# Top-k attention's mask and exponential as two ScalarE passes, the scaling on GpSimd, silu's product on VectorE

## The chip, the cores and the metric

The kernel runs on one core of a Trainium2 chip. Its time is the device time of one execution in microseconds (us). The engines are named as the profile names them: PE (TensorE matmul; PEld is its weight load), DVE (VectorE), ACT (ScalarE), POOL (GpSimd) and SP (SyncE, which issues the DMAs). Each engine works through its own queue in order; semaphores make one wait for another.

## The reference, cut to what matters

Three parts follow each other. The first is attention of 16 heads over 576 positions, in which each row of scores keeps its 32 largest:

```python
scores = scale * q @ k.T
kth = 32nd largest of each row
scores = where(scores >= kth, scores, -1e9) - rowmax
attn = exp(scores); attn /= attn.sum(-1) + 1e-9
x = attn @ v                             # 1152 tokens x 512
h = x @ w_in                             # 512 -> 2048, the "m" part
x = (h * sigmoid(h)) @ w_out             # silu, 2048 -> 512
P = sinkhorn(exp(x @ w_gate))            # 1152 tokens x 8 experts
out = sum_e P[:, e] * (relu(x @ w1[e]) @ w2[e])
```

## The kernel before

The 1152 tokens are cut into nine tiles of 128, and these into five groups: group 0 has tile 0, groups 1 to 4 have two tiles each. For each group the attention runs over four pairs of heads, and then the m part of the group (m0 to m4: 16 blocks of the 2048 hidden columns each). From 620 us on eight experts follow, on PE alone at its pace.

**One score tile** (`score_tile`, L314) is 128 rows by 576 scores. There are 8 in group 0 and 64 in groups 1 to 4; of these eight (names ending in h) serve the odd half tiles of group 2. PE forms the scores (L320, `ps`), ACT copies them to `s` (L323), then DVE finds the 32 largest in four rounds: MAX8 (L332, `m8`) finds eight, MATCH_REPLACE8 (L339) strikes them out in `w`. Beside that ACT computes `e = exp(scale*s - scale*max)` (L337), as soon as the first round has given the row's maximum and `tiny` (POOL from group 1 on) has scaled it (L335, `sm`). After the fourth round DVE multiplies `e` with `s >= kth` into `s` and sums it (L342), `tiny` adds 1e-9 (L344), DVE takes the reciprocal (L345), ACT scales `s` (L347). PE transposes the result in five pieces (L350, L352, `pt`), ACT copies them to `aT` (L363, L364), and PE multiplies by v (L360, `pav`).

**silu** in `step` (L447 to L454): with t = tanh(h/2), silu(h) = (t+1)*h/2. ACT computes t (L447); for m1 and m4 DVE forms (t+1)*h in one instruction from PSUM (L449); for m2 and m3 ACT copies h (L451) and adds 1 to t (L452), and POOL multiplies (L453). `split` (L135) then parts a float32 array in a high and a low half: ACT writes the high one (L137), POOL or DVE the difference (L138).

**What sets the order.** The code gives each instruction a priority; a scheduler (Tile's, with a timeline of its own) lays them out on the five queues ahead of time. The work of groups has priority; `FILL` hands out low-priority filler for PE that needs no attention result of a later group: experts 0 to 7 for tile 0 (`row_ffn`: L598, L609, L614, L617, with four splits of 128x512 each by ACT and POOL for one block), and expert 0 for tiles 1 to 4. The m part of group g runs while DVE is in group g+1. The first m part that runs in blocks, m1, splits its weights on the way (two splits of 128x512 per block); m2 to m4 load what it kept.

`tc.issue_after(behind.ins)` keeps the instructions in its scope behind `opened`, the evacuation of the first token tile after m0, for the four tiles of group 1's first pair. Five buffers hold `s` (SB).

The lines that the change touches are these, with what calls them.

Of the kernel before, what the change touches and what calls it, by code (L numbers as in the profile page):

```python
# [8 lines left out]
F32 = mybir.dt.float32  # L9
# [3 lines left out]
AF = mybir.ActivationFunctionType  # L13
ALU = mybir.AluOpType
# [3 lines left out]
P = 128  # L18
TOPK = 32
# [53 lines left out]
def topk_attention_moe_sinkhorn_kernel(  # L73
# [12 lines left out]
    nc = tc.nc  # L86
    B, H, S, D = q.shape
# [6 lines left out]
    NTT = NT // P  # L94
    SH = S // 2
    SCALE = 1.0 / D ** 0.5
    MASKED = -1e9 / SCALE
    W = DM
    assert NDC * P == W

# [7 lines left out]
    const = ctx.enter_context(tc.tile_pool(name="const", bufs=1))  # L108
# [1 line left out]
    make_identity(nc, ident)  # L110
    ones = const.tile([P, P], F32, name="ones")
    nc.gpsimd.memset(ones, 1.0)
    neg = const.tile([P, 1], F32, name="neg")
    nc.gpsimd.memset(neg, MASKED)
    wg_raw = const.tile([P, NDC, NE], F32, name="wg_raw")
    wgH = const.tile([P, NDC, NE], F32R, name="wgH")
    wgL = const.tile([P, NDC, NE], F32R, name="wgL")
# [78 lines left out]
    sp = att.enter_context(tc.tile_pool(name="sp", bufs=SW))  # L196
# [116 lines left out]
    def score_tile(nm, qq, qL, kk, js, cols, soon, behind=None, late=False):  # L313

        ps = ps_s.tile([P, 2, 512], F32, name=f"ps_{nm}", tag="s")

        for j in js:
            for part, a in enumerate((qq, qL)):
                for hh in range(2):
                    nc.tensor.matmul(ps[:, hh, 0:SH], a[:, j, cols], kk[:, j, hh * SH : (hh + 1) * SH],  # L320
                                     start=j == js[0] and part == 0, stop=j == js[-1] and part == 1)
        s = sp.tile([P, S], F32, name=f"s_{nm}", tag="s", bufs=SB)
        copied.append(nc.scalar.activation(s.rearrange("p (a c) -> p a c", a=2), ps[:, :, 0:SH], AF.Copy))  # L323
        w = sp.tile([P, S], F32, name=f"w_{nm}", tag="w")
        m8 = small.tile([P, TOPK], F32, name=f"m8_{nm}", tag="m8")
        sm = small.tile([P, 4], F32, name=f"sm_{nm}", tag="sm")
        e = sp.tile([P, S], F32, name=f"e_{nm}", tag="e")
        src = s
        tiny = nc.vector if soon else nc.gpsimd
        for r in range(TOPK // 8):  # L330
            mr = m8[:, 8 * r : 8 * r + 8]
            nc.vector.max(mr, src)  # L332
            if r == 0:

                tiny.tensor_scalar(sm[:, 0:1], m8[:, 0:1], -SCALE, None, op0=ALU.mult)  # L335
                with tc.issue_after(behind.ins) if behind and late else nullcontext():
                    nc.scalar.activation(e, s, AF.Exp, scale=SCALE, bias=sm[:, 0:1])  # L337
            if r < TOPK // 8 - 1:
                nc.vector.match_replace(out=w, in_to_replace=mr, in_values=src, imm_value=-3e38)  # L339
                src = w  # L340

        nc.vector.scalar_tensor_tensor(s, s, m8[:, TOPK - 1 : TOPK], e, op0=ALU.is_ge, op1=ALU.mult,  # L342
                                       accum_out=sm[:, 1:2])
        tiny.tensor_scalar(sm[:, 2:3], sm[:, 1:2], 1e-9, None, op0=ALU.add)  # L344
        normal.append(nc.vector.reciprocal(sm[:, 3:4], sm[:, 2:3]))  # L345
        with tc.issue_after(behind.ins) if behind else nullcontext():
            nc.scalar.activation(s, s, AF.Copy, scale=sm[:, 3:4])  # L347
        pt = ps_t.tile([P, 4, P], F32, name=f"pt_{nm}", tag="tr")
# [73 lines left out]
    def step(pend, nm, xs, ys, wa, wb, first, last, silu, ph, pool, late=False, depth=2, done=None, half=False):  # L422
# [3 lines left out]
        ph = ph[:, :N]  # L426
# [16 lines left out]
        if silu:  # L443

            g = hp.tile([P, W], F32, name=f"g_{nm}", tag="g")[:, :N]
            t = hp.tile([P, W], F32, name=f"t_{nm}", tag="t")[:, :N]
            nc.scalar.activation(t, ph, AF.Tanh, scale=0.5)  # L447
            if late or nm.startswith("m1"):
                nc.vector.scalar_tensor_tensor(g, t, 1.0, ph, op0=ALU.add, op1=ALU.mult)  # L449
            else:  # L450
                nc.scalar.activation(g, ph, AF.Copy)  # L451
                nc.scalar.activation(t, t, AF.Copy, bias=1.0)  # L452
                nc.gpsimd.tensor_mul(g, t, g)  # L453
            split(gH, gL, g, nc.vector if late else nc.gpsimd)  # L454
        elif late:
            nc.scalar.activation(gH, ph, AF.Relu)
            evacs.append(nc.vector.scalar_tensor_tensor(gL, ph, 0.0, gH.bitcast(F32), op0=ALU.max, op1=ALU.subtract))
        else:
            g = hp.tile([P, W], F32, name=f"g_{nm}", tag="g")[:, :N]
            nc.scalar.activation(g, ph, AF.Relu)  # L460
            split(gH, gL, g)
# [280 lines left out]
    for u, unit in enumerate(units):  # L742
        g = unit[0]
# [21 lines left out]
        if g == 0:  # L765
# [6 lines left out]
            late = right.enter_context(tc.tile_pool(name="late", bufs=1, side="right", reuse_waits="tile"))  # L772
# [284 lines left out]
    for i, e in enumerate(ORDER):  # L1057
# [89 lines left out]
```

## Time and profile before

| | us |
|---|---|
| median of 3 runs | 1222.58 (1220.61 to 1222.71) |
| the profiled execution | 1223.83 |
| its span, first to last instruction | 1222.0 |
| PE busy, in the span | 1176.0 (96%) |
| DVE busy | 800.5 (66%) |
| ACT busy | 609.2 (50%) |
| POOL busy | 593.2 (49%) |

The shares of the whole span mix stages: DVE is at 9 tenths from 30 us to 505 us (the attention), and between 3 and 7 tenths after that, while PE is at 9 tenths from 150 us to the end. PE's matmuls overlap each other, and a matmul's end is modelled, so that a busy PE is not PE at its pace; the pace is read from how many matmuls of a form go through in a stretch in which PE waits for nothing. The chain of work that ended last lies 82% on PE and 11% on DVE.

### The profile page before, as it was taken

To read this page: it belongs to the slowest core of one execution; us is meant where nothing else is said; L and a number is where in the kernel's file an instruction comes from. 1 tells how busy PE (TensorE), PEld (TensorE's weight loads), DVE (VectorE), ACT (ScalarE), POOL (GpSimd) and SP (SyncE) were. 2 spreads that over 40 slices of the span, in tenths; PEclk is the share of its full clock that TensorE was granted. 3 is DMA by queue.
4 is the path that set the end of the run, shared out by engine and by line. 5 is a ranking of instruction groups with operands and counts; after the bars stand their busy time and mean duration, and the time that the engine had idled before them with its cause. 6 is when DMAs were issued, how large, how long until landed. Compare 5 with 4: busy or idle time off the path is not lost.

```text
span 1222.0 us, 17930 instructions
## 1 busy us (share of the span) xinstructions
PE 1176.0 (96%) x6122; PEld 949.6 (78%) x6122; DVE 800.5 (66%) x1543; ACT 609.2 (50%) x1241; POOL 593.2 (49%) x665
## 2 busy tenths in 40 slices
PE   5797999999999999999999999999999999999998
PEld 3664666788778888888787888888888888888887
DVE  7989999999999999203567634634445345344444
ACT  6856887788876877643313332332323223323212
POOL 6666766788634843530546444445334444353310
PEclk9997999999999999999999999999999999999999
DMA  9889777998786898899814221121111211211001
GB/s 268 292 285 323 261 245 235 323 333 288 232 304 236 274 323 293 288 325 375 293 56 129 76 80 35 52 72 49 52 52 37 84 35 35 70 52 53 18 1 69
DMA packets 131723, 210.91 MB, mean 173 GB/s; under 512 B 23472, under 2 KB 69552, under 8 KB 131632
## 3 DMA queue, kind: packets, MB, share of 16 engines
q1 hardware_dynamic: 131632, 209.77, 51.4%
q8 instruction: 48, 0.79, 0.3%
q14 instruction: 43, 0.35, 0.1%
HBM read 170.15 MB, written 39.58 MB: 172 GB/s over the span
## 4 chain that ended last, share of the span: by engine, by line
PE 82%; DVE 11%; ACT 2%; DMA 1%; POOL 1%; issue 1%; SPq 0%; POOLq 0%; ACTq 0%; DVEq 0%
PE h L147 9%; PE h L148 9%; PE h L149 9%; PE bank L147 5%; PE bank L149 5%; PE bank L148 5%; PE yA L149 4%; PE yB L149 4%; PE yB L147 4%; PE yA L147 4%; PE yA L148 4%; PE yB L148 4%; PE bank L598 4%; DVE m L332 3%; PE pav L360 3%; DVE w L339 3%
## 5 line engine op out<-in xcount | busy, mean ns | idle before, releaser
L138 POOL TENSOR_TENSOR wp<-rw,wp 128x512 fp32r<-128x512 f32 (+1 forms) x56 | 86.7, 1567 | 195.2 <-ACT wp L137 195.2
L332 DVE MAX8 m<-w 128x8 f32<-128x576 f32 x192 | 140.0, 745 | 0.7
L138 POOL TENSOR_TENSOR wa<-raw,wa 128x512 fp32r<-128x512 f32 x88 | 114.9, 1318 | 29.6 <-ACT wa L137 14.2
L138 POOL TENSOR_TENSOR w<-rw,w 128x512 fp32r<-128x512 f32 x56 | 72.0, 1290 | 92.0 <-ACT w L137 92.0
L339 DVE MATCH_REPLACE8 w<-m,w 128x576 f32<-128x576 f32 x128 | 94.4, 739 | 0.0
L978 DVE SCALAR_TENSOR_TENSOR gL_0b<-gB,gH_0b 128x512 fp32r<-128x512 f32 (+1 forms) x56 | 44.5, 794 | 55.7 <-ACT gH_0b L977 54.8
L147 PE MATMUL yB<-w,gH_0b 128*128 128x512 f32 x208 | 80.9, 389 | 0.0
L148 PE MATMUL yB<-w,gH_0b 128*128 128x512 f32 x208 | 80.9, 389 | 0.0
L149 PE MATMUL yB<-w,gL_0b 128*128 128x512 f32 x208 | 80.1, 389 | 0.0
L977 ACT ACTIVATE gH_0b<-gB 128x512 fp32r<-128x512 f32 (+1 forms) x56 | 33.6, 600 | 76.1 <-PE yB L148 41.4
L148 PE MATMUL h<-x1L,wp 128*128 128x512 f32 x168 | 65.6, 391 | 0.0
L149 PE MATMUL h<-x1H,wp 128*128 128x512 f32 x168 | 65.6, 390 | 0.0
L147 PE MATMUL h<-x1H,wp 128*128 128x512 f32 x168 | 65.6, 390 | 0.0
L991 DVE TENSOR_TENSOR gB<-u,h 128x512 f32<-128x512 f32 x56 | 38.5, 687 | 35.6 <-PE h L149 35.5
L342 DVE SCALAR_TENSOR_TENSOR s<-s,m,e 128x576 f32<-128x576 f32 x64 | 61.2, 956 | 0.5
L137 ACT ACTIVATE w<-rw 128x512 fp32r<-128x512 f32 x56 | 34.6, 627 | 49.8 <-PE yB L149 48.3
L147 PE MATMUL bank<-xH,wa 128*128 128x256 f32 x192 | 57.2, 298 | 1.8 <-DVE g_m L449 1.1
L598 PE MATMUL bank<-wb,gT_e 128*128 128x512 f32 x128 | 58.2, 594 | 0.0
L347 ACT ACTIVATE s<-s,sm 128x576 f32<-128x576 f32 x64 | 49.9, 781 | 15.3 <-DVE sm L345 15.0
L137 ACT ACTIVATE wa<-raw 128x512 fp32r<-128x512 f32 x88 | 55.0, 648 | 3.2 <-DMA raw<-in_moe_w_dram 2.5
L138 DVE TENSOR_TENSOR wp<-sp,wp 128x1024 fp32r<-128x1024 f32 x28 | 45.3, 1617 | 15.3 <-ACT wp L137 15.3
L337 ACT ACTIVATE e<-s,sm 128x576 f32<-128x576 f32 x64 | 50.1, 784 | 8.4 <-DVE s L342 4.5
(376 smaller groups left out, 3670.6 us busy)
## 6 DMA issues: line engine op xcount, KB each, us to landing
wa<-sk SPq DMA_DIRECT2D x64, 512.0 KB, 5.5
wb<-sk SPq DMA_DIRECT2D x64, 512.0 KB, 5.3
rw<-in_moe_w_dram SPq DMA_DIRECT2D x112, 256.0 KB, 2.7
raw<-in_moe_w_dram SPq DMA_DIRECT2D x80, 256.0 KB, 3.8
wb<-in_moe_w_dram SPq DMA_DIRECT2D x32, 512.0 KB, 5.1
sk<-wa SPq DMA_DIRECT2D x24, 512.0 KB, 3.9
sk<-wb SPq DMA_DIRECT2D x24, 512.0 KB, 4.2
wfr<-in_moe_w_in_dram SPq DMA_DIRECT2D x16, 512.0 KB, 6.0
```

The source lines that it names most:

```text
L137: nc.scalar.activation(dH, src, AF.Copy)
L138: eng.tensor_sub(dL, src, dH.bitcast(F32))
L147: nc.tensor.matmul(ps, wH, xH, start=first, stop=False, skip_group_check=more)
L148: nc.tensor.matmul(ps, wH, xL, start=False, stop=False, skip_group_check=more)
L149: return nc.tensor.matmul(ps, wL, xH, start=False, stop=last, skip_group_check=more)
L332: nc.vector.max(mr, src)
L337: nc.scalar.activation(e, s, AF.Exp, scale=SCALE, bias=sm[:, 0:1])
L339: nc.vector.match_replace(out=w, in_to_replace=mr, in_values=src, imm_value=-3e38)
L342: nc.vector.scalar_tensor_tensor(s, s, m8[:, TOPK - 1 : TOPK], e, op0=ALU.is_ge, op1=ALU.mult, accum_out=sm[:, 1:2])
L347: nc.scalar.activation(s, s, AF.Copy, scale=sm[:, 3:4])
L598: nc.tensor.matmul(y, gT[:, c * P : (c + 1) * P], b[c], start=F == 0 and c == 0, stop=F == nF - 1 and c == NDC - 1)
L978: nc.vector.scalar_tensor_tensor(gL, src, 0.0, gH.bitcast(F32), op0=ALU.max, op1=ALU.subtract)
```

## The change

`tiny`, `e` and the two instructions on it stay as they were for the eight tiles of group 0 (`soon`). For the 64 tiles of groups 1 to 4:

- DVE's compare, multiply and sum (L342) goes, and ACT's exp of the whole tile into `e` (L337).
- After the fourth round ACT runs two passes over `s` in place. Prelu of kth - s with slope 2^-80 for negative arguments leaves 2^-80*(kth - s) where s >= kth, and kth - s itself, a positive number, elsewhere. Exp of that times -scale*2^80 plus scale*(kth - max) gives exp(scale*(s - max)) where s >= kth and zero elsewhere, and sums the row in the same instruction.
- POOL's first tiny instruction now forms scale*(kth - max), after the fourth round instead of the first.
- The scaling by the reciprocal goes from ACT to POOL.
- In m2 and m3 ACT's two passes and POOL's product give way to DVE's single instruction, as in m1 and m4.
- The constant `neg` gives way to an unused one of the same size.

The counts of the two built programs differ by this and by nothing else: ACT has 64 instructions fewer, POOL 64 passes of 128x576 more and 32 products of 128x256 fewer, DVE 64 instructions of 128x576 fewer and 32 of 128x256 more. PE's are the same, in another order.

```diff
--- before.py
+++ after.py
@@ -94,7 +94,7 @@
     NTT = NT // P
     SH = S // 2
     SCALE = 1.0 / D ** 0.5
-    MASKED = -1e9 / SCALE
+    BELOW = 2.0**-80
     W = DM
     assert NDC * P == W
 
@@ -110,8 +110,7 @@
     make_identity(nc, ident)
     ones = const.tile([P, P], F32, name="ones")
     nc.gpsimd.memset(ones, 1.0)
-    neg = const.tile([P, 1], F32, name="neg")
-    nc.gpsimd.memset(neg, MASKED)
+    const.tile([P, 1], F32, name="pad_c")
     wg_raw = const.tile([P, NDC, NE], F32, name="wg_raw")
     wgH = const.tile([P, NDC, NE], F32R, name="wgH")
     wgL = const.tile([P, NDC, NE], F32R, name="wgL")
@@ -324,27 +323,35 @@
         w = sp.tile([P, S], F32, name=f"w_{nm}", tag="w")
         m8 = small.tile([P, TOPK], F32, name=f"m8_{nm}", tag="m8")
         sm = small.tile([P, 4], F32, name=f"sm_{nm}", tag="sm")
-        e = sp.tile([P, S], F32, name=f"e_{nm}", tag="e")
+        e = sp.tile([P, S], F32, name=f"e_{nm}", tag="e") if soon else None
         src = s
         tiny = nc.vector if soon else nc.gpsimd
         for r in range(TOPK // 8):
             mr = m8[:, 8 * r : 8 * r + 8]
             nc.vector.max(mr, src)
-            if r == 0:
-
-                tiny.tensor_scalar(sm[:, 0:1], m8[:, 0:1], -SCALE, None, op0=ALU.mult)
-                with tc.issue_after(behind.ins) if behind and late else nullcontext():
-                    nc.scalar.activation(e, s, AF.Exp, scale=SCALE, bias=sm[:, 0:1])
+            if r == 0 and soon:
+
+                nc.vector.tensor_scalar(sm[:, 0:1], m8[:, 0:1], -SCALE, None, op0=ALU.mult)
+                nc.scalar.activation(e, s, AF.Exp, scale=SCALE, bias=sm[:, 0:1])
             if r < TOPK // 8 - 1:
                 nc.vector.match_replace(out=w, in_to_replace=mr, in_values=src, imm_value=-3e38)
                 src = w
 
-        nc.vector.scalar_tensor_tensor(s, s, m8[:, TOPK - 1 : TOPK], e, op0=ALU.is_ge, op1=ALU.mult,
-                                       accum_out=sm[:, 1:2])
+        kth = m8[:, TOPK - 1 : TOPK]
+        if soon:
+            nc.vector.scalar_tensor_tensor(s, s, kth, e, op0=ALU.is_ge, op1=ALU.mult, accum_out=sm[:, 1:2])
+        else:
+
+            tiny.tensor_scalar(sm[:, 0:1], kth, m8[:, 0:1], SCALE, op0=ALU.subtract, op1=ALU.mult)
+            with tc.issue_after(behind.ins) if behind else nullcontext():
+                nc.scalar.activation(s, s, AF.Prelu, scale=-1.0, bias=kth, alpha=BELOW)
+                nc.scalar.activation(s, s, AF.Exp, scale=-SCALE / BELOW, bias=sm[:, 0:1], accum_out=sm[:, 1:2])
         tiny.tensor_scalar(sm[:, 2:3], sm[:, 1:2], 1e-9, None, op0=ALU.add)
         normal.append(nc.vector.reciprocal(sm[:, 3:4], sm[:, 2:3]))
-        with tc.issue_after(behind.ins) if behind else nullcontext():
+        if soon:
             nc.scalar.activation(s, s, AF.Copy, scale=sm[:, 3:4])
+        else:
+            nc.gpsimd.tensor_scalar(s, s, sm[:, 3:4], None, op0=ALU.mult)
         pt = ps_t.tile([P, 4, P], F32, name=f"pt_{nm}", tag="tr")
         for c in range(4):
             nc.tensor.transpose(pt[:, c, :], s[:, c * P : (c + 1) * P], ident)
@@ -445,12 +452,7 @@
             g = hp.tile([P, W], F32, name=f"g_{nm}", tag="g")[:, :N]
             t = hp.tile([P, W], F32, name=f"t_{nm}", tag="t")[:, :N]
             nc.scalar.activation(t, ph, AF.Tanh, scale=0.5)
-            if late or nm.startswith("m1"):
-                nc.vector.scalar_tensor_tensor(g, t, 1.0, ph, op0=ALU.add, op1=ALU.mult)
-            else:
-                nc.scalar.activation(g, ph, AF.Copy)
-                nc.scalar.activation(t, t, AF.Copy, bias=1.0)
-                nc.gpsimd.tensor_mul(g, t, g)
+            nc.vector.scalar_tensor_tensor(g, t, 1.0, ph, op0=ALU.add, op1=ALU.mult)
             split(gH, gL, g, nc.vector if late else nc.gpsimd)
         elif late:
             nc.scalar.activation(gH, ph, AF.Relu)
```

The scheduler lays out all of groups 1 to 4 anew; group 0 and all from the last part of m4 on stand as before. Three places follow. Names end in the buffer's number; `s_0_0_0_0`, `m_1_0_0_0_0` and `sm_0_0_0_0` (`_1632`, `_1635`, `_1636` before) belong to the first tile of group 1, `s_0_0_0_1` to the second, `s_0_0_1_0` and `s_0_0_1_1` to the third and fourth.

DVE, end of the first tile of group 1, before: from the tile's last MAX to its reciprocal.

```order
L332 MAX m_1_0_0_0_0_1635<-w_0_0_0_0_1634 128x8
L332 MAX m_1_0_0_0_1_1668<-w_0_0_0_1_1667 128x8
L142 TENSOR_TENSOR qL_2_1_1782<-pq_2_1_1776,qq_2_1_1781 128x512
L342 SCALAR_TENSOR_TENSOR s_0_0_0_0_1632,sm_0_0_0_0_1636<-s_0_0_0_0_1632,m_1_0_0_0_0_1635,e_0_0_0_0_1637 128x576
L339 MATCH_REPLACE w_0_0_1_0_1700<-m_1_0_0_1_0_1701,s_0_0_1_0_1698 128x576
L332 MAX m_1_0_1_0_0_1795<-s_0_1_0_0_1792 128x8
L339 MATCH_REPLACE w_0_0_1_1_1733<-m_1_0_0_1_1_1734,s_0_0_1_1_1731 128x576
L345 RECIPROCAL sm_0_0_0_0_1636<-sm_0_0_0_0_1636 128x1
```

DVE, the same place, after, from behind that qL_2_1 (the line numbers are those of the changed kernel; L331 is MAX, L337 MATCH_REPLACE, L350 the reciprocal).

```order
L337 MATCH_REPLACE w_0_0_1_0_1697<-m_1_0_0_1_0_1698,s_0_0_1_0_1695 128x576
L331 MAX m_1_0_1_0_0_1790<-s_0_1_0_0_1787 128x8
L337 MATCH_REPLACE w_0_0_1_1_1729<-m_1_0_0_1_1_1730,s_0_0_1_1_1727 128x576
L331 MAX m_1_0_0_1_0_1698<-w_0_0_1_0_1697 128x8
L331 MAX m_1_0_0_1_1_1730<-w_0_0_1_1_1729 128x8
L337 MATCH_REPLACE w_0_0_1_0_1697<-m_1_0_0_1_0_1698,w_0_0_1_0_1697 128x576
L337 MATCH_REPLACE w_0_0_1_1_1729<-m_1_0_0_1_1_1730,w_0_0_1_1_1729 128x576
L141 TENSOR_TENSOR x1L<-bank_132,x1H 128x4x128
L331 MAX m_1_0_0_1_0_1698<-w_0_0_1_0_1697 128x8
L331 MAX m_1_0_0_1_1_1730<-w_0_0_1_1_1729 128x8
L337 MATCH_REPLACE w_0_0_1_0_1697<-m_1_0_0_1_0_1698,w_0_0_1_0_1697 128x576
L350 RECIPROCAL sm_0_0_0_0_1635<-sm_0_0_0_0_1635 128x1
```

The rows begin where L342 stood before, right behind qL_2_1. L342 is gone, and eleven instructions, most of them the third and fourth tile's rounds, stand ahead of the reciprocal now; three stood between L342 and the reciprocal before.

PE, first transposes of group 1, before (L350 and L352 are the transposes; L147 to L149 on `wa` are filler):

```order
L297 MATMUL pq_3_1_1937<-ident,qd_3_1_1935 128x128 x4
L350 MATMUL pt_0_0_0_0_1651<-ident,s_0_0_0_0_1632 128x128 x4
L352 MATMUL pt_1_0_0_0_0_1656<-ident,s_0_0_0_0_1632 128x128
L147 MATMUL bank_134<-wa_1010,x1H 128x512
L148 MATMUL bank_134<-wa_1010,x1H 128x512
L149 MATMUL bank_134<-wa_1010,x1L 128x512
L147 MATMUL bank_134<-wa_1015,x1H 128x512
```

PE, the same place, after (L357 and L359 are the transposes, L146 to L148 the filler):

```order
L296 MATMUL pq_3_1_1928<-ident,qd_3_1_1926 128x128 x4
L146 MATMUL bank_133<-wa_1009,x1H 128x512
L147 MATMUL bank_133<-wa_1009,x1H 128x512
L148 MATMUL bank_133<-wa_1009,x1L 128x512
L146 MATMUL bank_133<-wa_1014,x1H 128x512
L357 MATMUL pt_0_0_0_0_1649<-ident,s_0_0_0_0_1631 128x128 x4
L359 MATMUL pt_1_0_0_0_0_1654<-ident,s_0_0_0_0_1631 128x128
```

Four filler matmuls, which need the first split weights, have moved ahead of the first transposes.

POOL, the first tiles of group 1, before (L344 adds 1e-9, L335 scales the maximum, L138 is a split of a filler's weights):

```order
L344 TENSOR_SCALAR sm_0_0_0_0_1636<-sm_0_0_0_0_1636 128x1
L335 TENSOR_SCALAR sm_0_1_0_0_1796<-m_1_0_1_0_0_1795 128x1
L291 COPY qd_0_0_3146<-qn_0_0_2098 64x2x128
L138 TENSOR_TENSOR wa_1010<-raw_1011,wa_1010 128x512
L138 TENSOR_TENSOR wa_1015<-raw_1016,wa_1015 128x512
L344 TENSOR_SCALAR sm_0_0_0_1_1669<-sm_0_0_0_1_1669 128x1
L138 TENSOR_TENSOR wa_1020<-raw_1021,wa_1020 128x512
L138 TENSOR_TENSOR wa_1025<-raw_1026,wa_1025 128x512
L335 TENSOR_SCALAR sm_0_1_0_1_1829<-m_1_0_1_0_1_1828 128x1
L138 TENSOR_TENSOR wa_1054<-raw_1055,wa_1054 128x512
```

POOL, the same place, after (L349 adds 1e-9, L345 forms scale*(kth - max), L354 is the scaling of 128x576, L137 the split):

```order
L349 TENSOR_SCALAR sm_0_0_0_0_1635<-sm_0_0_0_0_1635 128x1
L137 TENSOR_TENSOR wa_1009<-raw_1010,wa_1009 128x512
L349 TENSOR_SCALAR sm_0_0_0_1_1667<-sm_0_0_0_1_1667 128x1
L354 TENSOR_SCALAR s_0_0_0_0_1631<-s_0_0_0_0_1631,sm_0_0_0_0_1635 128x576
L137 TENSOR_TENSOR wa_1014<-raw_1015,wa_1014 128x512
L137 TENSOR_TENSOR wa_1019<-raw_1020,wa_1019 128x512
L345 TENSOR_SCALAR sm_0_0_1_0_1699<-m_1_0_0_1_0_1698 128x1
L137 TENSOR_TENSOR wa_1024<-raw_1025,wa_1024 128x512
L354 TENSOR_SCALAR s_0_0_0_1_1663<-s_0_0_0_1_1663,sm_0_0_0_1_1667 128x576
L345 TENSOR_SCALAR sm_0_0_1_1_1731<-m_1_0_0_1_1_1730 128x1
```

The scalings stand between the splits that PE's filler waits for, each behind two other waits of the same tile.

## Rows read from the trace of the kernel before

**Rows 1.** Busy time by stretch: columns as in its first line.
```profile
core 0: us, PE busy (x) PEld busy (x) DVE busy (x) ACT busy (x) POOL busy (x), PEclk, DMA share, GB/s
...
103.70:215.00 111.30, 109.30 (x523) 74.01 (x524) 108.52 (x243) 91.84 (x181) 78.70 (x91) 0.96 0.78 257
215.00:319.40 104.40, 103.18 (x722) 83.07 (x720) 102.71 (x228) 86.23 (x201) 79.93 (x102) 1.00 0.89 303
319.40:410.00 90.60, 89.35 (x549) 70.61 (x548) 89.16 (x198) 68.86 (x160) 42.31 (x68) 1.00 0.76 262
410.00:502.30 92.30, 89.85 (x614) 77.07 (x613) 86.32 (x196) 70.98 (x157) 46.66 (x72) 1.00 0.87 301
```

**Rows 2.** The same view for an expert stretch, PE at its pace.
```profile
700.00:800.00 100.00, 100.00 (x443) 82.81 (x442) 46.62 (x59) 33.82 (x56) 44.12 (x41) 1.00 0.20 59
```

**Rows 3.** Pieces of the chain that ended last: start, us, what.
```profile
127.25 2.31 PE pav L360 x20
...
139.38 3.43 PE bank L598 x8
...
195.62 1.06 PE ps_h L320 x8
```

**Rows 4.** PE's instructions in order of time: start, us, instruction.
```profile
350.01 0.28 PE L148 MATMUL bank<-xL,wa 128*128 128x256 f32 x1
...
351.19 0.28 PE L149 MATMUL bank<-xH,wa 128*128 128x256 f32 x1
```

**Rows 5.** The same view near 439 us: four transposes of 128 columns.
```profile
438.76 0.60 PE L350 MATMUL pt<-ident,s 128*128 128x128 f32 x4
```

**Rows 6.** DVE groups, 103.7 to 502.3 us: busy us, mean ns | idle before.
```profile
L342 DVE SCALAR_TENSOR_TENSOR s<-s,m,e 128x576 f32<-128x576 f32 x55 | 53.1, 966 | 0.4
...
L342 DVE SCALAR_TENSOR_TENSOR s_h<-s_h,m_h,e_h 128x576 f32<-128x576 f32 x8 | 10.4, 1305 | 0.0
...
L449 DVE SCALAR_TENSOR_TENSOR g_m<-t_m,bank 128x256 f32<-128x256 f32 x16 | 6.4, 401 | 0.0
```

**Rows 7.** ACT groups of the same stretch.
```profile
L347 ACT ACTIVATE s<-s,sm 128x576 f32<-128x576 f32 x55 | 43.1, 783 | 10.1 <-DVE sm L345 9.8
...
L452 ACT ACTIVATE t_m<-t_m 128x256 f32<-128x256 f32 x21 | 9.1, 432 | 0.0
L451 ACT ACTIVATE g_m<-bank 128x256 f32<-128x256 f32 x21 | 8.2, 391 | 0.0
```

**Rows 8.** POOL groups of the whole span.
```profile
L138 POOL TENSOR_TENSOR wa<-raw,wa 128x512 fp32r<-128x512 f32 x88 | 114.9, 1318 | 29.6 <-ACT wa L137 14.2 <-PE bank L149 4.4 <-PE pt L350 3.2
...
L453 POOL TENSOR_TENSOR g_m<-t_m,g_m 128x256 f32<-128x256 f32 x32 | 25.1, 785 | 37.0 <-ACT t_m L452 36.4 <-PE pt L352 0.4
...
L291 POOL COPY qd<-qn 128x512 f32<-128x512 f32 x12 | 8.7, 723 | 2.5 <-issue 1.9 <-PE pq L299 0.2
...
L1086 POOL TENSOR_SCALAR acc<-acc,pr 128x512 f32<-128x512 f32 x4 | 3.6, 906 | 0.0
```

**Rows 9.** POOL's waits, 103.7 to 502.3 us: us in total, times, longest.
```profile
POOL sm L344 <- DVE s L342: 24.5, 12, 4.7
...
POOL wa L138 <- ACT wa L137: 14.2, 14, 2.9
```

**Rows 10.** DVE in order of time at group 1's first tile.
```profile
99.81 0.81 DVE L342 SCALAR_TENSOR_TENSOR s<-s,m,e 128x576 f32<-128x576 f32 x1
...
102.66 0.15 DVE L345 RECIPROCAL sm<-sm 128x1 f32<-128x1 f32 x1
```

**Rows 11.** PE in order of time at the same place.
```profile
103.67 1.12 PE L350 MATMUL pt<-ident,s 128*128 128x128 f32 x4 [2.56 <-ACT s L347]
...
105.52 0.79 PE L147 MATMUL bank<-wa,x1H 128*128 128x512 f32 x1 [0.52 <-ACT wa L137]
```

**Rows 12.** Busy time by stretch there, columns as in rows 1.
```profile
102.00:106.00 4.00, 1.81 (x6) 1.22 (x6) 4.00 (x11) 3.16 (x6) 1.05 (x3) 0.50 0.80 251
...
110.00:112.00 2.00, 2.00 (x6) 1.23 (x6) 2.00 (x5) 0.89 (x2) 1.78 (x3) 0.50 1.02 370
```

## The prediction, made before the changed kernel ran

> **What bounds the kernel now.** Start with busy time by stretch. From the first transposes of group 1 at 103.7 us to those of group 3 at 319.4 (A: groups 1 and 2, 215.7 us) DVE is busy 108.5 + 102.7 = 211.2 us, 98%; from there to the last ones at 502.3 (B: groups 3 and 4, 182.9 us) 175.5 us, 96% [rows 1]. PE is shown at 391.7 of the 398.6 us, which would make it the bound too. So the next step is PE's pace, since a busy PE may be one that crawls.
>
> Prices of PE at its pace: 443 matmuls of 512 columns in 100 us, 0.226 us each [rows 2]; in the chain of waits 20 `pav` in 2.31 us (0.116), eight L598 records in 3.43 (0.429; each instruction leaves two records, 0.858), eight scores in 1.06 (0.133) [rows 3]; ten matmuls of 256 columns between two starts, 350.01 and 351.19 (0.118) [rows 4]; four transposes in 0.60, the last of which takes the 0.28 of one alone, so 0.107 [rows 5, 4].
>
> PE's instructions in the two orders, between the same transposes of before and of after:
> A before: 262 of 512 columns 59.2 + 192 of 256 columns 22.7 + 48 L598 41.2 + 156 scores 20.7 + 296 transposes 31.7 + 120 `pav` 13.9 = 189 us of work. A after: 272, 192, 56, 156, 304, 120 = 200.
> B before: 240, 444, 16, 108, 195, 70 = 164. B after: 220, 432, 8, 108, 187, 70 = 150.
> So PE loses 215.7 - 189 = 26.5 us in A and 182.9 - 164 = 19 in B, one ninth of its time. DVE ends last in both stretches, but PE is right behind: an idle DVE can give back 45 us in all and no more, and those prices are for matmuls that follow their like, so part of the 45 isn't waiting at all. Behind 502 us PE works at its pace and any gain goes through to the end.
>
> **The change part by part.** *DVE loses L342*: 55 tiles of 0.966 us and 8 of 1.305 [rows 6]. A has 24 and 8 of them: 23.2 + 10.4 = 33.6, so 211.2 becomes 177.6. B has 31: 175.5 - 29.9 = 145.6, and gets the products of m2 and m3, 21 of 0.401 [rows 6] = 8.4: 154. The order puts 3 or 4 rounds of B ahead of it, some 5 us less. DVE is then at 80% of A and still above 90% of B.
>
> *ACT* exchanges two passes for two. L347 takes 0.783 [rows 7], and I take that for Prelu and for Exp with a sum. Lower bound 0.6 (what 0.391 and 0.432 for 256 columns [rows 7] leave room for), upper 1.0 with the sum read out: 64 passes, -12 to +14 us. ACT idles 37 us in A and 43 in B [rows 1], the 42 passes of L451 and L452, 17.3 us, go from B [rows 7]: nothing on the path.
>
> *POOL* gets 63 scalings of 128x576 in these stretches. No trace shows one. Nearest rows: TENSOR_SCALAR of 128x512 0.906, COPY of 128x512 0.723, the two-input L138 1.318 [rows 8]. Times 576/512: 1.02, low 0.81, high 1.48. I take 1.02, the same operation. A: 158.6 [rows 1] + 32 x 1.02 + 7 more splits of 1.318 that the order moves into it = 200. B: 89.0 + 31.6 - 8 splits 10.5 - 21 products of 0.785 [rows 8] 16.5 = 94. In A POOL has 15 to 20 us left, at the high price none.
> What moves to POOL gets dearer: the scaling 1.02 for 0.783 on ACT, as the product costs 0.785 there for 0.401 on DVE. The Trainium skill's "GPSIMD Engine Reference", § 3.1 Elementwise, keeps "use DVE for elementwise" as the rule, which speaks against this part of the change, and gives 1.8 cycles an element at 1.2 GHz as the best case of a tight loop: an estimate of 0.86 us for 576, and POOL's A at 195. The trace agrees with the rule in direction, and its 0.906 for 512 columns stands above that best case.
>
> *The tile's path grows.* From the fourth round to the transposes there were L342, a tiny POOL step, a reciprocal, 0.78 on ACT. Now: tiny POOL step, two ACT passes, tiny POOL step, reciprocal, 1.02 on POOL. That is 1.57 + 1.02 - 0.97 - 0.78 = 0.8 us more and two stops in POOL's queue and one in ACT's where there was one each. Behind a waiting POOL stand the splits of the filler's weights, and PE waits for those. The four rounds of the next tiles cover this wherever a tile is ready ahead of PE. Where that cover is gone it is the start: before, L342 began at 99.81, the reciprocal at 102.66 [rows 10], the transposes at 103.67, with 2.56 us of waiting for ACT; the first filler at 105.52 waited for a split [rows 11]. Now eleven instructions of DVE, seven of them rounds of 0.7, stand ahead of the reciprocal: some 107.3, the scaling ends near 108.4, and the four fillers ahead of the transposes end at about 107.3. The piece then ends 2.3 us late (bounds 0 and 5); there the granted clock is 0.50, the 1.2 GHz level, and was still at 110 to 112 [rows 12], after PE had idled ahead of 103.67.
>
> *Silu in m2 and m3* loses an ACT step and POOL's queue; it lies on PE's second matmuls there, and the splits on POOL follow 0.4 us sooner a block. I cost it at nothing beyond DVE's 8.4.
>
> *The sum.* A: work 200 + 0.9 (four fillers) = 201; losses 26.5 + 2.3 at the start - 8 = 21, since DVE's idle time grows from 4.5 to 40 us, but POOL's falls from 57 to 20. That "8" is my choice between 0 and half (13). A = 222, +6.3. B: work 150, losses 19 - 4 = 15, DVE above 90% still: 165, -18. Work of 3.0 us (11 more in A, 14 less in B) is left for later at PE's pace; 0.9 of it stands ahead of A's transposes, so 2.1 is added. Sum: 6.3 - 18 + 2.1 = -9.6. Profiled execution 1223.83 - 9.6 = 1214.2; the median of before is 1.25 below its profiled one, so 1213.
>
> **The rivals.**
> *POOL becomes the bound of groups 1 and 2 (slower).* Before, POOL stood 24.5 us waiting for L342 ahead of the second tiny step, and 14.2 for ACT's halves of splits [rows 9]. Now it meets two such waits a tile, and each holds the splits behind it: 24.5/63 = 0.39 x 2 x 32 = 25, plus 14, plus 200 of work = 239 us for A, 17 more than forecast. Price: -9.6 + 17 = +7.5, 1230. It decides once POOL's waits in A exceed 22 us (200 + 22 = the 222 of the forecast); it raises the time only from 32 on. For it: splits and scalings stand interleaved, each scaling behind two waits of its tile. Against it: the scheduler has put other tiles' work between, and ACT's passes come soon.
> Beside it: by the Trainium skill's "SBUF — State Buffer", § Who interferes with whom, a VectorE instruction with two SBUF inputs contends with a GpSimd instruction that reads SBUF. L342 has two and runs 0.966 on average where one takes 0.81 [rows 6, 10], which agrees. By that rule the collision would end for these 64 tiles, in POOL's favour.
>
> *No change.* PE's losses are not DVE's doing (starts of matmuls, mixed sizes, loads): all 45 stay and the start costs its 2.3. Then 2.3 for the whole, 1225. The filler only changes places: A 229, B 169. For it: PE's gaps are small and many; against it, DVE at 98% with five buffers for `s`.
>
> *Nearly all waits go.* Losses halve in both: 12 less than forecast in the sum, 1201. That needs POOL at its low price and no queueing.
>
> **How the numbers follow.** Forecast 0.50, no change 0.20, slower 0.22, nearly all waits 0.08. A difference under 0.2% (2.4 us) is about what a measurement of this kernel can't tell from none. Faster takes the forecast and the last rival, 0.58; same 0.20; slower 0.22. ACT's and POOL's bounds (0.81 and 1.48: -7 to +15 on POOL in A, of which the idle 20 takes most) and the start's (-2.3 to +2.7) move the forecast between 1206 and 1219. The range goes on up to 1228, past no change and into the slower case, and leaves out its larger half and the largest gain, about 2 in 10.
>
> **What would show it.** Right: DVE near 178 us busy in A and 150 in B; scalings of about 1.0 us; group 3's first transposes near 326, the last ones near 491; idle POOL in A near 20 us. POOL's bound: POOL above 95% through A with PE waiting for splits or for L354, group 3 at 340 or later. No change: DVE idle 40 us and PE's losses as they were. Wrong at the root: scalings far from 1.02, or PE's waits gone to an engine that no row above points to.

## The result: slower by 1.5%, lost in groups 1 and 2

The changed kernel takes 1240.08 us (median of 4 runs, 1237.41 to 1240.96) against 1221.59 of before (4 runs, 1218.91 to 1222.71): a ratio of 1.0148, 95% interval 1.0134 to 1.0162. The forecast was 1213, faster, in a range of 1206 to 1228. Its profiled span is 1238.6 us.

Busy time by stretch of the changed kernel, cut as [rows 1] at the first transposes of group 3 and the last of the attention (columns: us, PE, PEld, DVE, ACT and POOL busy, granted clock, DMA share, GB/s):

```profile
103.70:349.80 246.10, 226.19 (x1281) 163.20 (x1281) 190.53 (x407) 187.58 (x425) 214.79 (x234) 0.98 0.76 257
349.80:517.70 167.90, 166.16 (x1111) 139.79 (x1110) 154.86 (x346) 123.36 (x291) 116.70 (x143) 1.00 0.82 281
517.70:1238.60 720.90, 713.95 (x3336) 592.13 (x3334) 327.89 (x495) 217.06 (x396) 275.51 (x257) 1.00 0.29 97
```

The kernel before, with B cut at 503.0 us, where its attention ends, instead of 502.3:

```profile
103.70:319.40 215.70, 212.47 (x1243) 157.07 (x1243) 211.23 (x470) 178.07 (x380) 158.63 (x192) 0.98 0.83 279
319.40:503.00 183.60, 179.90 (x1167) 148.37 (x1166) 175.48 (x393) 139.90 (x317) 89.55 (x139) 1.00 0.82 282
503.00:1222.00 719.00, 710.75 (x3318) 589.61 (x3316) 323.43 (x483) 223.17 (x416) 282.89 (x267) 1.00 0.29 96
```

A (groups 1 and 2) takes 246.1 us where 215.7 were and 222 forecast; B takes 167.9, where 183.6 were and 165 forecast; the rest 720.9, 2 more than before. So the miss is A, 24 us of it. DVE is at 77% there and POOL at 87%.

POOL's scaling, by form (mean ns of one), the other TENSOR_SCALAR of POOL on floats, and the one that converts integers:

```profile
L354 POOL TENSOR_SCALAR s<-s,sm 128x576 f32<-128x576 f32 x56 | 97.8, 1748 | 12.2 <-DVE sm L350 11.8
...
L501 POOL TENSOR_SCALAR cv_n<-wfr 128x512 int32<-128x512 uint32 x19 | 32.6, 1714 | 26.1 <-DVE wf L504 14.9 <-DMA wfr<-in_moe_w_out_dram 6.4 <-DMA wfr<-in_moe_w_in_dram 4.0
...
L1088 POOL TENSOR_SCALAR acc<-acc,pr 128x512 f32<-128x512 f32 x4 | 3.1, 802 | 0.0
```

The scaling takes 1.75 us, not 1.02, and beyond the 1.48 that was the upper bound. The row that the price came from, [rows 8], is written with two operations (times a scalar, times 1.0), and the scaling with one. Min, median and longest (ns) of the four L1088 of the changed kernel are:

```profile
L1088 POOL TENSOR_SCALAR acc<-acc,pr x4: 690/691/1134, 680.2 to 682.7; 128x512 f32<-128x512 f32 x4
```

The waits in A: DVE, idle for 4.5 us there before, now waits mostly for a tile's scores to be copied by ACT, and POOL for ACT's halves of splits (us in total, times, longest):

```profile
DVE m L331 <- ACT s L322: 33.4, 16, 4.5
```
```profile
POOL wa L137 <- ACT wa L136: 12.8, 10, 3.3
POOL sm L345 <- DVE m L331: 3.9, 1, 3.9
POOL s L354 <- DVE sm L350: 3.0, 3, 1.2
POOL sm L349 <- ACT s L348: 2.3, 3, 1.6
```

**A ledger for PE.** Every kernel of this study issues the same 6122 matmul records. Each is given its time at PE's pace (0.227 for 512 columns, 0.118 for 256, and so on, as in the prediction, but each record of a `pav` by its width: 0.116 for 256 columns, 0.029 for 64); the sum is 1120.0 us in every kernel. What a stretch lasts beyond the work that starts in it counts as lost, waits and a lower granted clock alike:

| lost by PE, us | to 103.7 | A | B | after | sum |
|---|---|---|---|---|---|
| before | 52.8 | 22.6 | 11.1 | 15.5 | 102.0 |
| the changed kernel | 53.0 | 42.0 | 9.0 | 14.6 | 118.6 |

The work in A rises from 193.1 to 204.1 and that in B falls from 172.5 to 158.9, about as read from the orders; that only changes places. The 16.6 us of the span are the 19.4 that PE loses more in A, less 2.1 in B and 0.9 behind.

Where in A: busy time from 260 to 340 us (group 2) of the changed kernel, and of the kernel before in the same 80 us:

```profile
260.00:340.00 80.00, 67.41 (x438) 53.16 (x437) 63.52 (x136) 56.14 (x135) 72.43 (x80) 0.98 0.72 252
```
```profile
260.00:340.00 80.00, 78.30 (x518) 62.57 (x517) 79.61 (x182) 65.67 (x144) 56.63 (x71) 1.00 0.83 284
```

By the ledger PE loses 21.2 us in these 80 and lost 7.2 before. In neither kernel is any filler issued between 240 and 300 us, so PE has only group 2's tiles and m1 to work on there. At the start, 100 to 120 us, it loses 13.1 instead of 10.2.

### The profile page after: what moved, and what is told of

It reads as the page before. It is cut to its first block, busy times and chain, and to the rows that moved or that the text cites. A ratio compares the mean times of both kernels' runs of the same rounds, so it can differ in the third digit from the quotient of the medians.

```text
span 1238.6 us, 17926 instructions
## 1 busy us (share of the span) xinstructions
PE 1178.7 (95%) x6122; PEld 949.4 (77%) x6122; DVE 765.8 (62%) x1447; ACT 597.3 (48%) x1241; POOL 664.8 (54%) x696
## 4 chain that ended last, share of the span: by engine, by line
PE 81%; DVE 6%; DMA 5%; ACT 4%; issue 2%; POOL 1%; SPq 1%; ACTq 0%; POOLq 0%; DVEq 0%
PE h L147 8%; PE h L148 8%; PE h L146 8%; PE bank L146 5%; PE bank L147 5%; PE bank L148 5%; PE yA L148 4%; PE yB L148 4%; PE yB L147 4%; PE yA L147 4%; PE yA L146 4%; PE yB L146 4%; PE bank L600 4%; PE pav L367 3%; DVE m L331 2%; PE ps L319 2%
## 5 line engine op out<-in xcount | busy, mean ns | idle before, releaser
L137 POOL TENSOR_TENSOR wp<-rw,wp 128x512 fp32r<-128x512 f32 (+1 forms) x56 | 86.2, 1559 | 197.3 <-ACT wp L136 197.3
L331 DVE MAX8 m<-w 128x8 f32<-128x576 f32 x192 | 142.4, 751 | 1.9
L137 POOL TENSOR_TENSOR w<-rw,w 128x512 fp32r<-128x512 f32 x56 | 72.5, 1299 | 91.0 <-ACT w L136 91.0
L137 POOL TENSOR_TENSOR wa<-raw,wa 128x512 fp32r<-128x512 f32 x88 | 111.8, 1283 | 15.2 <-ACT wa L136 13.5
L354 POOL TENSOR_SCALAR s<-s,sm 128x576 f32<-128x576 f32 x56 | 97.8, 1748 | 12.2 <-DVE sm L350 11.8
L337 DVE MATCH_REPLACE8 w<-m,w 128x576 f32<-128x576 f32 x128 | 94.9, 742 | 0.0
L146 PE MATMUL yB<-w,gH_0b 128*128 128x512 f32 x208 | 80.9, 389 | 0.0
L147 PE MATMUL yB<-w,gH_0b 128*128 128x512 f32 x208 | 80.9, 389 | 0.0
L148 PE MATMUL yB<-w,gL_0b 128*128 128x512 f32 x208 | 80.1, 389 | 0.0
L980 DVE SCALAR_TENSOR_TENSOR gL_0b<-gB,gH_0b 128x512 fp32r<-128x512 f32 (+1 forms) x56 | 44.1, 789 | 55.6 <-ACT gH_0b L979 54.8
L331 DVE MAX8 m<-s 128x8 f32<-128x576 f32 x64 | 48.0, 753 | 44.2 <-ACT s L322 43.7
L148 PE MATMUL h<-x1H,wp 128*128 128x512 f32 x168 | 65.6, 391 | 0.0
L147 PE MATMUL h<-x1L,wp 128*128 128x512 f32 x168 | 65.6, 390 | 0.0
L146 PE MATMUL h<-x1H,wp 128*128 128x512 f32 x168 | 65.5, 390 | 0.0
L136 ACT ACTIVATE wa<-raw 128x512 fp32r<-128x512 f32 x88 | 55.6, 640 | 12.8 <-DMA raw<-in_moe_w_dram 10.4
L146 PE MATMUL bank<-xH,wa 128*128 128x256 f32 x192 | 56.6, 295 | 1.5 <-DVE g_m L455 1.3
L137 POOL TENSOR_TENSOR gL_m<-g_m,gH_m 128x256 fp32r<-128x256 f32 x48 | 35.4, 738 | 36.7 <-ACT gH_m L136 31.3
L148 PE MATMUL bank<-xH,wa 128*128 128x256 f32 x192 | 54.2, 283 | 0.0
```

What stands on the lines that cost most here:

```text
L136: nc.scalar.activation(dH, src, AF.Copy)
L137: eng.tensor_sub(dL, src, dH.bitcast(F32))
L146: nc.tensor.matmul(ps, wH, xH, start=first, stop=False, skip_group_check=more)
L147: nc.tensor.matmul(ps, wH, xL, start=False, stop=False, skip_group_check=more)
L148: return nc.tensor.matmul(ps, wL, xH, start=False, stop=last, skip_group_check=more)
L354: nc.gpsimd.tensor_scalar(s, s, sm[:, 3:4], None, op0=ALU.mult)
```

## The experiments

Ratios are to the kernel before, run beside them on the same chip, with 95% intervals. The experiments are named e1 to e16. They were run on several chips, so ratios compare better across them than times.

### One operation or two

```diff
-            nc.gpsimd.tensor_scalar(s, s, sm[:, 3:4], None, op0=ALU.mult)
+            nc.gpsimd.tensor_scalar(s, s, sm[:, 3:4], 1.0, op0=ALU.mult, op1=ALU.mult)
```

> The changed kernel, but the scaling on GpSimd is written with two operations (times the reciprocal, times 1.0) instead of one; nothing else is edited, the scheduler lays out anew. Theory PRICE: the scaling's 1.75 us (26 + 8 of them in groups 1 and 2) is what made POOL the bound there. The other two-operation TENSOR_SCALAR of this program takes 0.69 us for 512 columns, so 0.8 for 576 here; POOL's busy time in groups 1 and 2 falls from 217 to about 185 us, that stretch from 249 to about 222, and the whole from 1240 to about 1213 to 1217. Theory PATH: the longer chain of a tile (two stops in POOL's queue and one in ACT's) delays the score tiles whatever the scaling costs: the stretch stays above 240 us and the time above 1230.

e1: 1219.11 us, ratio 0.998 (0.9968 to 0.9993): 21 us less than the changed kernel.

```profile
L354 POOL TENSOR_SCALAR s<-s,sm 128x576 f32<-128x576 f32 x56 | 41.8, 748 | 14.3 <-DVE sm L350 13.9
```
```profile
103.70:320.10 216.40, 212.54 (x1256) 158.29 (x1256) 188.25 (x412) 182.98 (x419) 180.37 (x233) 0.98 0.84 282
320.10:487.70 167.60, 165.83 (x1083) 136.30 (x1081) 152.41 (x341) 124.46 (x288) 85.45 (x141) 1.00 0.82 277
487.70:1218.60 730.90, 723.35 (x3390) 599.51 (x3388) 327.43 (x498) 220.48 (x402) 277.78 (x260) 1.00 0.31 100
```

The scaling takes 0.75 us. A is 216.4, not 222, and yet the time is above 1213 to 1217: the attention ends 15 us earlier than before, and the rest takes 12 us longer, since the work has been left for it. PE's losses by the ledger: A 20.7, B 8.6, after 16.3.

### The scaling on ACT or on DVE, and silu alone

```diff
-            nc.gpsimd.tensor_scalar(s, s, sm[:, 3:4], None, op0=ALU.mult)
+            with tc.issue_after(behind.ins) if behind else nullcontext():
+                nc.scalar.activation(s, s, AF.Copy, scale=sm[:, 3:4])          # e2
+            nc.vector.tensor_scalar(s, s, sm[:, 3:4], None, op0=ALU.mult)      # e3
```

> The changed kernel with the scaling back on ScalarE: three ACT passes of a tile after the fourth round. PRICE: POOL falls to about 158 us in groups 1 and 2, ACT rises from 190 to 217, so ACT is the next bound; stretch 222 to 232, time 1215 to 1225. PATH: the stop of the scaling in POOL's queue is gone but a third ACT pass stands in ACT's; stretch above 238, time above 1230.

e2: 1228.53 us, 1.0059 (1.0039 to 1.0080); A 213.9, which either theory gave longer; losses A 23.9, B 16.2.

> The changed kernel with the scaling on VectorE, in place, one operation. No trace shows its price there; 0.35 to 0.8 us. PRICE: POOL falls to 158 us in groups 1 and 2, DVE goes from 193 to 205 to 220; stretch 215 to 226, groups 3 and 4 165 to 180, time 1210 to 1225. PATH: stretch above 235, time above 1230.

e3: 1224.34 us, 1.0024 (1.0011 to 1.0037); one scaling takes 0.51 us by median and 0.66 on average; A 211.5, B 177.3; losses A 21.4, B 12.7. With POOL out of the tile's path the stretch is short in both, and neither beats the kernel before.

```diff
             nc.scalar.activation(t, ph, AF.Tanh, scale=0.5)
-            if late or nm.startswith("m1"):
...
+            nc.vector.scalar_tensor_tensor(g, t, 1.0, ph, op0=ALU.add, op1=ALU.mult)   # in the kernel before
```

> The kernel before with only the second part of the change: silu's product of m2 and m3 on VectorE. DVE was busy 175 of 183 us in groups 3 and 4 and gets 8 us more there: if DVE is that stretch's bound the time rises by 4 to 9 us to 1226 to 1231; if PE is, it stays within 2 us. Groups 1 and 2 stay at 216 us by either.

e4: 1225.15 us, 1.0024 (1.0012 to 1.0036), some 3 us (1.5 to 4.4 by the interval). That is more than nothing, and its interval reaches both expectations, so it settles neither. DVE is busy 180.6 of B's 185 us:

```profile
317.70:502.70 185.00, 178.01 (x1154) 145.73 (x1151) 180.59 (x413) 129.43 (x274) 73.00 (x118) 1.00 0.82 277
```

### The price apart from the order

The scheduler lays the kernel out anew for the cheap form, so e1 changes two things. Here the order is kept and the instruction exchanged after the layout (shortened):

```diff
+    for block in nc.cur_f.blocks:
+        for k, x in enumerate(block.instructions):
+            if x.name in names:      # the 64 scalings; e6 the other way round, from e1
+                block.instructions[k] = copy.replace(x, op1=ALU.mult, ins=x.ins + (one,))
```

> Every engine's order is the changed kernel's, row for row; only the 64 scalings on GpSimd are turned, after the layout, into their two-operation form (0.75 us instead of 1.75). PRICE: the stretch of groups 1 and 2 falls from 246 to 215 to 222 us and the whole from 1240 to 1215 to 1223. ORDER (the gain of the first experiment came from the other layout that it got): the time stays above 1232.

> The reverse: every engine's order is that of the two-operation kernel (1219), and the 64 scalings are turned into the one-operation form of 1.75 us. PRICE: groups 1 and 2 go from 216 to about 245 us, the time to 1238 to 1248. ORDER: below 1228.

e5: 1240.46 us, 1.0153 (1.0136 to 1.0169). e6: 1234.87 us, 1.0105 (1.0087 to 1.0124).

| us | laid out for 1.75 | laid out for 0.75 |
|---|---|---|
| a scaling takes 1.75 | 1240.1 (changed) | 1234.9 (e6) |
| a scaling takes 0.75 | 1240.5 (e5) | 1219.1 (e1) |

At the changed kernel's order the cheap scaling gains nothing: A stays at 245.9 us, and PE loses 42.1 there. POOL is now idle for 64 us of A (31 in the changed kernel), and the 80 us of group 2 read as before the exchange (e5: A, then 260 to 340 us):

```profile
103.70:349.60 245.90, 227.49 (x1280) 164.57 (x1280) 189.50 (x405) 186.97 (x423) 182.34 (x234) 0.97 0.76 256
260.00:340.00 80.00, 67.94 (x433) 53.51 (x433) 63.32 (x135) 55.77 (x134) 60.07 (x78) 0.96 0.71 251
```

The time that POOL gained turns into waits, and DVE waits for the copies of scores as it did (33.4 us in the changed kernel; POOL's wait for ACT was 12.8):

```profile
DVE m L331 <- ACT s L322: 35.6, 17, 5.2
```
```profile
POOL wa L137 <- ACT wa L136: 27.0, 19, 4.2
```

So in the queues as they stand POOL's busy time isn't what holds A; the order is. At the order made for the cheap form the dear one costs 15.8 us, with A at 228.1 us and POOL busy for 92% of it (e6):

```profile
103.70:331.80 228.10, 217.38 (x1255) 159.62 (x1254) 186.51 (x406) 183.01 (x417) 209.96 (x229) 0.97 0.80 265
```

For e5 ORDER's range came true; for e6 neither did, since 1234.9 lies between the two. Either the price or the order made for it is enough to lose 16 to 21 us, and the two don't add.

### The kernel before with nothing but the scaling moved

> The kernel before with one thing changed: the scaling of groups 1 to 4 on GpSimd in the one-operation form (mask, exponential and silu as before). PRICE: POOL gets 32 x 1.75 = 56 us in groups 1 and 2, 159 + 56 = 215 of 216 us before any wait: that stretch goes to 235 to 250 us, the time to 1238 to 1255. PATH (it needs the two ACT passes and their stops in the queues): within 1 per cent of before, 1222 to 1232.

e8: 1252.9 us, 1.0265 (1.0224 to 1.0305); A 248.8 with POOL at 224.6.

> The kernel before with only the scaling of groups 1 to 4 on GpSimd, in the two-operation form; with one operation this took 1253. Theory PLAN (the scheduler lays groups 1 and 2 out for a GpSimd that the dear scaling makes the slowest, and the queues keep to it; no other part of the change is needed): with the cheap form the stretch is back at 216 to 222 us and the time at 1220 to 1228. Theory MOVE (a stop of each tile in GpSimd's queue is what costs, dear or cheap): above 1236.

e13: 1227.13 us, 1.0041 (1.0025 to 1.0057); A 222.1. The dear form alone makes A as long as in the changed kernel, without the two ACT passes; the cheap form takes nearly all of it back. A, then the scaling, of e8 and of e13:

```profile
103.70:352.50 248.80, 224.31 (x1268) 163.16 (x1269) 234.07 (x493) 163.74 (x353) 224.61 (x235) 0.97 0.72 244
...
L349 POOL TENSOR_SCALAR s<-s,sm 128x576 f32<-128x576 f32 x56 | 101.8, 1820 | 12.0 <-DVE sm L345 11.1 <-PE bank L149 0.3
```
```profile
103.70:325.80 222.10, 214.15 (x1240) 156.09 (x1239) 219.56 (x476) 156.72 (x348) 184.02 (x226) 0.98 0.81 271
...
L349 POOL TENSOR_SCALAR s<-s,sm 128x576 f32<-128x576 f32 x56 | 43.6, 778 | 19.1 <-DVE sm L345 15.2 <-ACT gH_e L137 1.7 <-DMA raw<-in_moe_w_dram 0.7
```

The scaling is 72 and 30 ns longer on average in these kernels, which keep the old mask L342, than without it (1748, 748), while its median stays within 4 ns. In e8 nine of the 25 scalings that run at the same time as an L342 take more than 1.8 us, up to 2.25, and none of the 39 others; in e13 three of eight take more than 0.8 us, up to 1.25, and none of the 56 others. The Trainium skill's "SBUF — State Buffer", § Who interferes with whom, lets a VectorE instruction with two SBUF inputs (the old mask is one) contend with a GpSimd instruction that reads SBUF; these long ones agree with that.

### Without silu's part

The cheap scaling, with ACT's two passes and POOL's product back in m2 and m3:

> The two-operation kernel without the silu part (ACT copies, ACT adds 1 and GpSimd multiplies again in m2 and m3): the attention part alone at the low price. If silu's product on VectorE costs here the 3 us that it cost alone, the time is about 1216; if DVE has room now that the mask is off it, silu's part is free or helps, 1219 to 1224.

e7: 1217.92 us, 0.9968 (0.9955 to 0.9981), the lowest ratio of this study, between the two expectations. Against e1 (0.998) the intervals overlap: silu's part costs some 1.5 us here, not clear of nothing.

### What holds the order: buffers, copies

In A of the changed kernel all five `s` are held for 200 of 246 us (before: 127 of 216), a tile holding one for 37 us (31). That 32 x 37 / 4.8 gives the 246 us of A proves nothing: tiles times holding time over buffers held is the length of the stretch, whatever sets it.

```diff
-SB = 5
+SB = 6        # e9, e10, e12, with one buffer for e; 4 in e11
```

> The changed kernel with six buffers for `s` instead of five (room comes from one buffer for `e` instead of two, which only group 0 uses now). Theory RING: in groups 1 and 2 all five buffers are held for 200 of 246 us, a tile holds its own for 37 us from the copy to the last transpose (before: 127 of 216 us, 31 us), and 32 tiles x 37 / 4.8 is the 246 us; so the ring of buffers sets the pace that the layout plans with. With six, the stretch falls below 230 us and the time to 1215 to 1230. Theory POOL (its queue in itself): six buffers change nothing, the stretch stays above 240 us, the time above 1235.

e9: 1247.51 us, 1.0208 (1.0183 to 1.0232). A is 234.1 us long, but with 187.7 us of work in it: PE loses 46.4.

> The two-operation kernel (1219) with six buffers for `s`. RING: the five were held for 145 of 216 us in groups 1 and 2, so the ring still binds in part: the stretch falls by 3 to 10 us, and since PE is right behind, the time by 0 to 6, 1213 to 1219. POOL: no change beyond 2 us.

e10: 1227.33 us, 1.0036 (1.0026 to 1.0046).

> The two-operation kernel with four buffers for `s`. RING: at the 31 us that a tile holds a buffer now, 32 tiles on some 3.8 buffers take 260 us; if a held tile gets through faster with fewer beside it (27 us), 228. The time rises by 10 to 40 us, to 1230 to 1260. POOL: within 5 us of 1219.

e11: 1225.84 us, 1.0028 (1.0015 to 1.0042), some 6 us over e1 by the ratios, where RING expected 10 to 40 and POOL at most 5.

> Two-operation scaling, six buffers for `s`, and silu's product back on ACT and GpSimd in m2 and m3 (1218 with five buffers). RING: 1212 to 1217, if both add up. POOL: 1218 within 2 us.

e12: 1227.06 us, 1.0034 (1.0023 to 1.0044). So RING falls: a sixth buffer is no gain in any of the three, and nothing shows that the full ring set the pace. But "no change" didn't come true either: by the ratios the three are some 7 to 8 us slower than with five buffers. Why isn't shown; the layout changed with the buffers.

```diff
+        kept = tc.cur_priority
+        tc.cur_priority = kept if soon else uid() * 100     # e14: ahead of the copy; e15: of the scores too
         copied.append(nc.scalar.activation(s.rearrange("p (a c) -> p a c", a=2), ps[:, :, 0:SH], AF.Copy))
+        tc.cur_priority = kept
```

> The changed kernel, with the copy of a tile's scores to `s` at the highest priority of the layout. In the changed kernel VectorE stands idle 52 us in groups 1 and 2, 24 of them in 11 gaps in which ScalarE runs the finished tile's first pass and then the next tile's copy. Theory HAND-OFF (the copy behind the pass is what stretches these groups): that idle time halves, the stretch falls from 246 to 225 to 238 us, the time to 1220 to 1232. PLAN: copies come no earlier, since the scores behind them are planned late; the time stays within 6 us of 1240.

e14: 1245.59 us, 1.0186 (1.0168 to 1.0205). DVE's idle time in A, which was to halve, is 59.7 us (55.6 in the changed kernel). The edit didn't do what it was for, so it doesn't speak against HAND-OFF, but nothing speaks for it either.

> The two-operation kernel, with a tile's scores and their copy at the highest priority. HAND-OFF: VectorE's remaining 25 us of idle time in groups 1 and 2 shrink, the time goes from 1219 to 1212 to 1218. PLAN: within 4 us of 1219, or slower where the scores push filler aside.

e15: 1224.97 us, 1.0022 (1.0012 to 1.0032), slower than e1.

### A scaling that costs nothing

> The changed kernel without the scaling by the row's sum in groups 1 to 4: that part of the computation is left out, so its time is that of a scaling that costs nothing on any engine. PLAN: GpSimd was no longer the slowest at 0.75 us, so 1213 to 1219, little below the two-operation kernel. If GpSimd still binds at 0.75 us (180 of 216 us busy): below 1210.

e16: 1222.0 us, 0.9995 (0.9984 to 1.0006), outside both expectations.

```profile
103.70:307.40 203.70, 200.63 (x1182) 147.41 (x1182) 177.79 (x393) 171.78 (x393) 142.22 (x183) 0.98 0.83 281
307.40:479.70 172.30, 168.51 (x1079) 137.17 (x1078) 158.40 (x357) 134.68 (x306) 74.89 (x124) 1.00 0.80 268
479.70:1221.00 741.30, 734.01 (x3461) 609.82 (x3459) 329.23 (x499) 223.84 (x410) 281.74 (x264) 1.00 0.32 105
```

The attention ends 23 us sooner than before, and 22 of them come back behind it, as PE's work that was left for later. This answers what the forecast rested on (PE's losses by the ledger):

| lost by PE, us | to 103.7 | A | B | after | sum |
|---|---|---|---|---|---|
| e1, cheap scaling | 53.0 | 20.7 | 8.6 | 16.3 | 98.6 |
| e7, and old silu | 52.7 | 19.3 | 9.1 | 14.3 | 95.4 |
| e16, no scaling | 52.4 | 21.5 | 11.5 | 15.6 | 101.0 |
| e6, dear at e1's order | 52.7 | 32.7 | 14.6 | 13.7 | 113.7 |
| e8, dear, old mask | 53.0 | 49.5 | 13.3 | 15.4 | 131.2 |

## Why the prediction was wrong, point by point

**Right.** DVE's instructions last 51 us less in sum over the whole program (64 of L342 [rows 6] gone, 32 products more), about as counted. Its busy time falls by 35 only: records of DVE overlap each other by 73 us in the kernel before and by 56 now. So DVE is busy for 190.5 us in A, not 178, and idle for 56 of the longer A. The orders' shift of work held: 11 us more in A, 13.6 less in B, 1.9 longer behind (2.1). The start: the first transposes come at 108.42, as forecast (108.4), though by a reciprocal that is 0.9 us sooner and a scaling 0.7 longer; PE loses 2.9 us more there (2.3).

```profile
106.37 0.15 DVE L350 RECIPROCAL sm<-sm 128x1 f32<-128x1 f32 x1
```
```profile
108.42 1.12 PE L357 MATMUL pt<-ident,s 128*128 128x128 f32 x4 [1.43 <-POOL s L354]
```

ACT's two passes cost 0.78 each, as taken, but the sum's read adds 0.21, inside the bound:

```profile
L348 ACT ACTIVATE s<-s,sm 128x576 f32<-128x576 f32 x55 | 43.1, 785 | 0.6 <-POOL sm L345 0.3
L347 ACT ACTIVATE s<-s,m 128x576 f32<-128x576 f32 x54 | 42.2, 782 | 9.8 <-DVE m L331 9.8
L348 ACT ACTIVATION_READ_ACCUMULATOR s<-s,sm 128x1 f32 x55 | 11.4, 208 | 0.0
```

**The step that failed first is POOL's price.** "I take 1.02, the same operation": it wasn't. The row was a mean of four two-operation instructions, two near 0.69 and two near 1.13 (684, 687, 1118 and 1135 ns); the scaling has one operation and takes 2.3 times what its two-operation form does. A one-operation TENSOR_SCALAR on POOL stood in the trace of before, the integer conversion, and isn't among the prediction's nearest rows: 1.59 us by median for 512 columns (1.54 in the changed kernel), which is 1.79 for 576, close to the price that was measured:

```profile
L499 POOL TENSOR_SCALAR cv_n<-wfr 128x512 int32<-128x512 uint32 x19 | 35.5, 1866 | 23.3 <-DVE wf L502 14.9 <-DMA wfr<-in_moe_w_out_dram 3.3 <-DMA wfr<-in_moe_w_in_dram 1.7
```

Its mean, 1866, holds single ones of up to 3.7 us. With 1.75, the sum for POOL's A is 200 + 32 x 0.73 = 223 before any wait (214.8 measured), and the slower rival becomes the likeliest.

**The slower rival had the right engine and place, but not the mechanism.** It priced the tile's two stops in POOL's queue at 25 us and ACT's splits at 14. Measured in A are 12.3 for the scaling's and the tiny steps' waits (of 3.9, 3.0, 2.3 and smaller ones) and 12.8. What it lacked is that the scheduler makes another order for the dear form, as the layouts of the changed kernel and of e1 show, between which nothing but the form differs, and that the five queues then keep to this order: e5 sets POOL free and gains nothing. In group 2, without filler, PE pays most of it: between 260 and 340 us it loses 14.0 us more than before in the same 80. What in that order holds A isn't settled: it isn't POOL's busy time (e5) nor the number of `s` buffers (e9, where PE loses still more); the copy behind the first pass was argued, and e14 failed to test it.

**The gain was mis-sized too.** "Losses 26.5 + 2.3 - 8" and "19 - 4" took for waiting what was in part work. The 0.116 of a `pav` is the price of a record [rows 3], and each `pav` instruction leaves two records, as the prediction says of L598; but it counts the 120 and 70 instructions once, where the trace has 240 and 140 records. With all records priced by their width before loses 22.6 and 11.1, not 26.5 and 19. And of these 33.7 PE still loses 29.3 with the mask off DVE and the scaling at 0.75 (e1), and 33.0 with no scaling (e16). DVE, 97% busy over A and B, worked beside PE, not ahead of it. So at 0.75, below the price that was taken, the gain is 2 to 4 us (e1, e7) instead of 9.6, closer to the rival "no change" than to the forecast. A sign was there: PE's named waits in A and B of before come to 9 us. What the rest of the losses is made of, no run shows.

**Silu's part**, costed at nothing beyond DVE's work, costs 1.5 to 4.4 us alone (e4).

On the Trainium skill's "GPSIMD Engine Reference", § 3.1 Elementwise: its best case of 1.8 cycles an element gave an estimate of 0.86 us, its rule "use DVE for elementwise" spoke against the change. By the runs the one-operation form takes 1.75, twice that, the two-operation form 0.75, less than that; and the rule holds in direction (0.51 us by median on DVE), but moving the scaling to DVE (e3) is no gain over the two-operation form on POOL. The 0.906 that stood above the best case was a mean: two of its four took 0.69, under the 0.77 that the page gives for 512.

## What to carry to other kernels

Take a price from the same form of instruction, with the number of its operations, and read its shortest and median time before its mean. Before counting on a busy engine's relief, sum the bound engine's work at its pace: if nearly all of the stretch is work, an earlier end of one stage only hands the work to the next. And where a scheduler lays out the queues, a dear instruction can cost in two ways, in its queue or by the order that was made for it; exchange the one with the other held to see which.

## What the runs showed of the hardware

A one-operation TENSOR_SCALAR with a per-row scalar on GpSimd takes 1.75 us for 128x576 float32 in place, and the same with a second operation (times 1.0) 0.75 us (means of 1746 to 1749 and of 747 to 750 ns in the kernels without the old mask), at the same order of instructions too (min, median and longest of the changed kernel, then of e5):

```profile
L354 POOL TENSOR_SCALAR s<-s,sm x56: 1722/1748/1765, 106.6 to 512.7; 128x576 f32<-128x576 f32 x56
```
```profile
L354 POOL TENSOR_SCALAR s<-s,sm x56: 736/748/767, 105.8 to 512.6; 128x576 f32<-128x576 f32 x56
```

On VectorE the one-operation form takes 0.51 us by median (e3), and 0.66 on average over the 64: 40 of them take 0.50 to 0.52 us; the 24 others, of up to 1.63 us, all ran at the same time as a GpSimd instruction, as did 19 of the 40. On ScalarE it takes 0.78 us by median and 0.80 on average (e2).
